# An FFT filter with a mixture of experts behind it: the first block's transposes ordered behind slot 29 of the opening plan

## The chip, the cores and the metric

The kernel runs on one core of a Trainium2 chip. Five engines work in that core, each on an instruction stream of its own, in order: TensorE (PE: matmuls, and transposes as matmuls), VectorE (DVE), ScalarE (ACT), GpSimd (POOL), and SyncE (SP), which here issues nearly all DMAs. An instruction that waits holds up everything behind it on its engine. The metric is the device time of one launch in microseconds; lower is better.

## The reference

Two parts, one after the other. First a spectral filter over the sequence, for 8 batches of 2496 tokens with 256 channels; then a mixture of experts over all 19968 tokens, in which each token goes to two of eight experts:

```python
X = np.fft.rfft(x, axis=1)
Y = X * (filt_r + 1j * filt_i)[None]
x = np.fft.irfft(Y, n=2496, axis=1).reshape(19968, 256)
logits = x @ w_gate
noisy = logits + np.log1p(np.exp(x @ w_noise)) * noise
top2 = two largest of the 8 noisy logits, softmax over the two -> weights
for e in range(8):                       # the tokens that chose e
    h = np.maximum(x[mask] @ w1[e], 0)   # 256 -> 1024
    out[mask] += weight * (h @ w2[e])    # 1024 -> 256
```

## The kernel before

**The filter.** 2496 = 39 x 64, so the transform is two DFTs: one over a (39 points) and one over b (64 points), each a matmul with a table of cosines and sines. One batch passes through `s1` (DFT over a, written to a DRAM scratch `fd`, lines 307 to 327 and 355), `kgl`/`kg0` (reads `fd` back), `kg1` (DFT over b and the product with the filter), `kg2` (inverse over b, into the tile `G`), `t3` (transposes `G`) and `i2` (inverse over a). `i2` (lines 503 to 526) is a matmul (L512) into a PSUM bank, a copy on ScalarE into a tile `yt` (L522), and a DMA of that tile into the DRAM tensor `y` (L526). Each half of a batch's channels takes six such rounds.

**Routing.** From `G` come the gate's logits; `gate` (VectorE, L725 to L827) finds each token's two experts and its rank in the list of each, with three small matmuls (L782 to L784) that need the sums `rs` (L766); `route` writes lists of token rows to DRAM, per expert.

**The experts.** A block is 512 tokens of one expert. `read_list` loads its row numbers, `gather` fetches the rows from `y` with four indirect DMAs on GpSimd (L991), `turn` transposes them: for each half kc of the 256 channels four transposes into one PSUM bank (`xps`, L1007), a copy on ScalarE (L1011) and a difference on VectorE (L1012). Then follow the two layers (lines 120 to 122), whose results are added to `out` by indirect DMAs.

**The order.** Two batches are filtered alone, by a plan written out in slots (`fft_stream`, 32 of them); every instruction of the plan is pinned to the one before it on its engine (`pin`), so that the plan stands in the order written. Slots 26 to 31 also hold the third batch's DFT over a (`s1`, two matmuls of it in each). The experts' blocks start once the first batch is routed, and their instructions are not pinned: the scheduler that builds the program places them between the plan's by its own estimate of times. From then on the generator of the filter and that of the experts run in turn. In the plan's last slots `t3` and `i2` of the second batch share two PSUM banks (tag `yps`, `MOVES[26]`). The first channel half writes its rounds through three tiles in turn, the second half through two:

```python
            yt = P.tile([RP, 4, 128], F32, name="yt", tag=("mxl0", "mxh1", "mxl1")[g0 // 4 % 3], bufs=1)
        else:
            yt = P.tile([RP, 4, 128 + E], F32, name="yt", bufs=2)
```

Outside the functions below, the plan's `s1` entries are these two lines (slot 26 to 31, and what `s1` runs):

```python
        for j in range(11):
            at(26 + j // 2, s1, 22 + j)
```

Of the kernel before, what the change touches and what calls it, by code (L numbers as in the profile page):

```python
# [124 lines left out]
def f32v(ap):  # L125
    return ap.bitcast(F32)
# [3 lines left out]
PACES = 115  # L130
FILL = {0: 0, 1: 14}
RAW = 3
WIDE = 4
FIRSTS = 2
EARLY = {"q1": "hps", "q2": "hps", "q5": "yps", "q6": "yps", "u1": "xps"}
# [5 lines left out]
class Moe:  # L141
    def __init__(self, ctx, tc, io):
        self.tc, self.nc, self.io = tc, tc.nc, io
        nc = self.nc
        self.cp = ctx.enter_context(tc.tile_pool(name="cp", bufs=1))
        self.dp = ctx.enter_context(tc.tile_pool(name="dp", bufs=1, space=DRAM))
        self.y = self.dp.tile([NROW, YW], F32, name="y")
        self.lst = self.dp.tile([NLR, LR], F32, name="lst")
        self.P = ctx.enter_context(tc.tile_pool(name="P", bufs=1))
        self.PS = ctx.enter_context(tc.tile_pool(name="PS", bufs=1, space=PSUM))  # L150
        self.xx, self.early, self.last = {}, True, {}
        self.writes, self.reads = [], []
        self.held = self.held_any = False
        self.banks = dict(EARLY)
        self.setup()
        self.tabs, self.wodd = [], 0
        self.sp = self.spw = self.lasta = None

    def after(self, i):
        return self.tc.issue_after(i.ins) if i is not None else nullcontext()  # L160
# [146 lines left out]
    def s1(self, bt, g0):  # L307
# [4 lines left out]
        x = self.xx.pop((bt, g0))  # L312
        if self.early and bt < RAW:

# [213 lines left out]
    def fft_stream(self):  # L528
# [48 lines left out]
        q = [(n, kg) for n in range(2 * FIRSTS) for kg in range(5)]  # L577
# [56 lines left out]
        for t in range(max(plan) + 1):  # L634
            self.banks.update(MOVES.get(t, {}))
            for g in plan.get(t, []):
                self.pin(g, hold=g.func is not gates)
            if t - 12 in start:
                gating.append(start.index(t - 12))
            if gating:  # L640
                self.pin(self.gating_more, gating[0], hold=False)
                if gating[0] in self.routes:
                    for _ in range(6):
                        self.pin(self.gating_more, gating[0], hold=False)
                    gating.pop(0)

            while self.done_routes < 0 and t >= 14:
                next(rq, None)
            yield -1

        while self.made < 1:
# [346 lines left out]
    def turn(self, xg, nt):  # L998

        nc, P = self.nc, self.P  # L1000
        xT = []
        xg, at = xg
        w = 128 * nt
        for kc in range(2):
            q = self.PS.tile([128, 512], F32, name="xps", bufs=1)
            for t in range(nt):
                nc.tensor.transpose(q[:, t * 128:(t + 1) * 128], xg[t][:, kc * 128:(kc + 1) * 128], self.ident)  # L1007
            h = P.tile([128, 512], R32, name=f"mxh{kc}", bufs=1)
            l = P.tile([128, 512], R32, name=f"mxl{kc}", bufs=1)
            h, l = h[:, :w], l[:, :w]  # L1010
            nc.scalar.copy(h, q[:, :w])  # L1011
            nc.vector.tensor_sub(l, q[:, :w], f32v(h))  # L1012
            xT.append((h, l))
        gate = P.tile([128, 4, 1], F32, name="gt", bufs=3)[:, :nt]
        rows = self.stage[:, 2048:2048 + 8 * YW].rearrange("p (s w) -> p s w", w=YW)[:, at:at + nt, D:]
        nc.gpsimd.tensor_copy(gate, rows[:, :, bass.ds(self.ra, 1)])
        xT.append(gate)
        return xT
# [48 lines left out]
    def expert(self, parts, may, fill=None):  # L1067
# [5 lines left out]
        while self.ahead:  # L1073
# [34 lines left out]
            for t in range(nt):  # L1108


                wide = ready >= WIDE
                if wide or t % 2 == 0:
# [130 lines left out]
```

## Time and profile before

| | |
|---|---|
| median of 3 runs | 2326.6 us (2326.11 to 2327.73) |
| the profiled execution | 2317.03 us, its span 2315.2 us |
| PE busy | 2264.9 us (98%), 13089 matmuls |
| DVE, ACT, POOL busy | 1542.5 (67%), 1189.4 (51%), 937.2 us (40%) |
| mean DMA rate | 142 GB/s; 239 GB/s from 115 to 160 us |
| PE busy from 115 to 160 us | 33.92 of 45 us |

Times in the rows are microseconds from the start of the span. A timeline row gives the start, the time until its last instruction ended, the engine, the line, the operation and what it writes and reads; in brackets stands how long the engine sat idle before it and what ended that. A row of waits gives who waited for whom, the sum, how often, and the longest. `SPq` is SyncE issuing a DMA: its duration is that of the issue, not of the transfer.

### The profile page before, as it was taken

The numbers are of one execution on the slowest core, as the hardware profiler recorded it, in microseconds if no ns is written. First come the engines' busy times: TensorE is split into PE (matmuls) and PEld (weight loads), VectorE is DVE, ScalarE is ACT, GpSimd is POOL, SyncE is SP. The second block draws the span as 40 slices with busy tenths as digits, with TensorE's granted clock in tenths as the row PEclk, the third lists the DMA queues.
The fourth block names the chain that finished last, engine by engine and source line by source line (L and its number), as shares of the span: only waits on it lengthen the run. The fifth ranks groups of instructions, "written<-read, shape, count | busy, mean of one in ns | idle before, by whom it ended". The sixth has DMA issues, their size and how long they took to land. (4 is left out here: it accounts for less than half of the span.)

```text
span 2315.2 us, 39310 instructions
## 1 busy us (share of the span) xinstructions
PE 2264.9 (98%) x13089; PEld 1898.8 (82%) x13089; DVE 1542.5 (67%) x3331; ACT 1189.4 (51%) x2373; POOL 937.2 (40%) x827
## 2 busy tenths in 40 slices
PE   8879999999999999999999999999999999999998
PEld 5448888888888888888888888888888888889997
DVE  4867797678669665875669666854444445557886
ACT  5655656654554554454444444443444344447775
POOL 4014254332435334443434433543535454535442
PEclk9989999999999999999999999999999999999999
DMA  8677757664655555554454553443444445567773
GB/s 238 193 236 193 195 139 200 175 160 120 180 132 130 142 130 131 118 147 120 106 131 104 117 143 87 95 100 88 95 90 94 90 93 128 124 185 224 216 218 87
DMA packets 284723, 329.64 MB, mean 142 GB/s; under 512 B 37371, under 2 KB 197603, under 8 KB 284515
## 3 DMA queue, kind: packets, MB, share of 16 engines
q1 hardware_dynamic: 222435, 241.61, 34.3%
q0 software_dynamic: 62080, 85.47, 21.5%
q8 instruction: 105, 1.72, 0.3%
q14 instruction: 103, 0.84, 0.1%
HBM read 221.98 MB, written 105.78 MB: 142 GB/s over the span
## 5 line engine op out<-in xcount | busy, mean ns | idle before, releaser
L1119 PE MATMUL yps<-w,hh 128*128 128x512 f32 x2112 | 747.3, 398 | 0.0
L1127 POOL DMA_INDIRECT out<-stage,ids x320 | 532.3, 1663 | 264.6 <-DVE stage L1126 121.3
L1120 PE MATMUL yps<-w,hl 128*128 128x256 f32 x2112 | 571.3, 281 | 0.0
L991 POOL DMA_INDIRECT stage<-y,ids x320 | 329.6, 1030 | 584.8 <-PE xps L1007 197.6
L121 PE MATMUL hps<-mxl,w1h 128*128 128x512 f32 (+1 forms) x1424 | 535.0, 376 | 0.0
L122 PE MATMUL hps<-mxh,w1l 128*128 128x512 f32 (+1 forms) x1424 | 528.8, 372 | 0.0
L1095 DVE SCALAR_TENSOR_TENSOR hl<-hps,hh 128x512 fp32r<-128x512 f32 (+1 forms) x712 | 438.6, 630 | 134.6 <-ACT hh L1094 133.2
L120 PE MATMUL hps<-mxh,w1h 128*128 128x512 f32 (+1 forms) x1424 | 523.1, 378 | 3.9 <-DVE hl L1095 3.3
L1094 ACT ACTIVATE hh<-hps 128x512 fp32r<-128x512 f32 (+1 forms) x712 | 381.5, 555 | 239.2 <-PE hps L122 230.2
L1119 PEld LDWEIGHTS yps<-w,hh 128*128 128x128 f32 x2112 | 389.3, 188 | 80.2 <-issue 0.2
L1120 PEld LDWEIGHTS yps<-w,hl 128*128 128x128 f32 x2112 | 397.1, 188 | 18.9 <-DVE w1l L1057 0.6
L122 PEld LDWEIGHTS hps<-mxh,w1l 128*128 128x128 f32 x1424 | 268.1, 188 | 46.7
L120 PEld LDWEIGHTS hps<-mxh,w1h 128*128 128x128 f32 x1424 | 264.9, 188 | 50.0 <-DVE hl L1095 6.5
L121 PEld LDWEIGHTS hps<-mxl,w1h 128*128 128x128 f32 x1424 | 268.2, 188 | 41.4
L1124 ACT ACTIVATE stage<-yps,gt 128x256 f32<-128x256 f32 x320 | 143.8, 476 | 273.0 <-PE yps L1120 235.9
L1126 DVE SCALAR_TENSOR_TENSOR stage<-yps,gt,stage 128x256 f32<-128x256 f32 x264 | 120.9, 479 | 184.6 <-ACT stage L1124 184.2
L1012 DVE TENSOR_TENSOR mxl<-xps,mxh 128x512 fp32r<-128x512 f32 (+1 forms) x178 | 113.0, 635 | 149.7 <-ACT mxh L1011 147.1
L1011 ACT CAST mxh<-xps 128x512 fp32r<-128x512 f32 (+1 forms) x178 | 96.8, 544 | 221.6 <-PE xps L1007 189.5
L963 POOL CAST ids<-lt 128x8 int32<-128x8 f32 (+2 forms) x63 | 15.3, 243 | 379.0 <-DMA lt<-lst 343.8
L1057 DVE TENSOR_TENSOR w1l<-stage,w1h 128x512 fp32r<-128x512 f32 x180 | 123.5, 686 | 58.4 <-ACT w1h L1056 56.6
L1056 ACT CAST w1h<-stage 128x512 fp32r<-128x512 f32 x180 | 111.8, 622 | 93.1 <-PE hps L121 51.8
L1057 DVE TENSOR_TENSOR w<-stage,w 128x512 fp32r<-128x512 f32 x216 | 141.8, 684 | 21.2 <-ACT w L1056 20.8
(222 smaller groups left out, 3075.9 us busy)
## 6 DMA issues: line engine op xcount, KB each, us to landing
stage<-w SPq DMA_DIRECT2D x396, 256.0 KB
x<-x SPq DMA_DIRECT2D x88, 256.0 KB
fd<-c SPq DMA_DIRECT2D x77, 240.0 KB
wb<-w SPq DMA_DIRECT2D x18, 1024.0 KB
fx<-fd SPq DMA_DIRECT2D x140, 128.0 KB
out<-z SPq DMA_DIRECT2D x24, 702.0 KB
y<-yt SPq DMA_DIRECT2D x40, 248.6 KB
y<-yt SPq DMA_DIRECT2D x40, 234.0 KB
```

What stands on the lines that cost most here:

```text
L120: nc.tensor.matmul(o, lh, rh, start=start, stop=False)
L121: nc.tensor.matmul(o, lh, rl, start=False, stop=False)
L122: nc.tensor.matmul(o, ll, rh, start=False, stop=stop)
L991: self.pin(lambda: self.nc.gpsimd.indirect_dma_start(out=x, out_offset=None, in_=self.y[:BLK + ready * ROWS], in_offset=bass.IndirectOffse ...
L1057: nc.vector.tensor_sub(l, sv, f32v(h))
L1094: nc.scalar.activation(h, p, AF.Relu)
L1095: nc.vector.scalar_tensor_tensor(l, p, 0.0, f32v(h), op0=ALU.max, op1=ALU.subtract)
L1119: nc.tensor.matmul(bank, h, hl, start=(f == 0), stop=False)
L1120: nc.tensor.matmul(p, l, hl[:, 0], start=False, stop=(f == 7))
L1124: nc.scalar.activation(o, p, AF.Copy, scale=gate[:, t])
L1126: nc.vector.scalar_tensor_tensor(o, bank[:, 1], gate[:, t], o, op0=ALU.mult, op1=ALU.add)
L1127: a = nc.gpsimd.indirect_dma_start(out=self.io["out"][:BLK + ready * ROWS], out_offset=bass.IndirectOffsetOnAxis(ap=ids[:, t:t + 1], axis= ...
```

## The change

The generator keeps the last matmul pinned at the end of slot 29 as `mark`. The first call of `turn` after that puts its first transpose behind `mark`, and clears it.

```diff
+TURN = 29
...
-        self.sp = self.spw = self.lasta = None
+        self.sp = self.spw = self.lasta = self.mark = None
...
             while self.done_routes < 0 and t >= 14:
                 next(rq, None)
+            if t == TURN:
+
+                self.mark = self.last[self.nc.tensor.engine]
             yield -1
...
             for t in range(nt):
-                nc.tensor.transpose(q[:, t * 128:(t + 1) * 128], xg[t][:, kc * 128:(kc + 1) * 128], self.ident)
+                with self.tc.issue_after(self.mark) if self.mark is not None else nullcontext():
+                    nc.tensor.transpose(q[:, t * 128:(t + 1) * 128], xg[t][:, kc * 128:(kc + 1) * 128], self.ident)
+                self.mark = None
```

Added lines move the numbers: L316, L491, L512 and L1007 of before are L317, L492, L513 and L1012 of the change. `q_1417` and the like are PSUM tiles.

TensorE's stream before, in slots 27 and 28 of the plan (L491 is `t3`, L512 `i2`, L316 `s1`), with the first block's transposes L1007 one by one among them:

```order
L512 MATMUL q_1412<-tf,cm 117x512
L1007 MATMUL xps<-ident,stage 128x128
L491 MATMUL q_1417<-ident,G 120x128 x4
L1007 MATMUL xps<-ident,stage 128x128
L512 MATMUL q_1424<-tf,cm 117x512
L316 MATMUL q_1429<-x,cm 120x512
L316 MATMUL q_1436<-x,cm 120x512
L491 MATMUL q_1442<-ident,G 120x128 x2
L1007 MATMUL xps<-ident,stage 128x128
L512 MATMUL q_1447<-tf,cm 117x512
L1007 MATMUL xps<-ident,stage 128x128
L491 MATMUL q_1452<-ident,G 120x128 x4
```

The same place in the change:

```order
L513 MATMUL q_1412<-tf,cm 117x512
L492 MATMUL q_1417<-ident,G 120x128 x4
L513 MATMUL q_1424<-tf,cm 117x512
L317 MATMUL q_1429<-x,cm 120x512
L317 MATMUL q_1436<-x,cm 120x512
L492 MATMUL q_1442<-ident,G 120x128 x2
L513 MATMUL q_1447<-tf,cm 117x512
L492 MATMUL q_1452<-ident,G 120x128 x4
```

All four transposes of the block's first half are gone from here; the plan's own matmuls stand as before.

Where they stand now, on TensorE at the end of slot 29 (q_1500 and q_1505 are its `s1`); first before:

```order
L512 MATMUL q_1494<-tf,cm 117x512
L316 MATMUL q_1500<-x,cm 120x512
L316 MATMUL q_1505<-x,cm 120x512
L491 MATMUL q_1510<-ident,G 120x128 x4
L512 MATMUL q_1517<-tf,cm 117x512
```

and in the change:

```order
L513 MATMUL q_1494<-tf,cm 117x512
L317 MATMUL q_1500<-x,cm 120x512
L317 MATMUL q_1505<-x,cm 120x512
L1012 MATMUL xps<-ident,stage 128x128 x4
L492 MATMUL q_1510<-ident,G 120x128 x4
L513 MATMUL q_1517<-tf,cm 117x512
```

The four stand together behind the slot's `s1`, ahead of slot 30. The second half's four transposes keep their place behind the first matmuls of the first block. The streams of ScalarE, GpSimd and SyncE are the same as before until about 165 us of the profiled execution, that of VectorE but for a few small swaps from about 144 us. Behind that the scheduler placed some instructions of the first blocks otherwise; TensorE's stream is the same again from its matmul 1413 of 13089, at about 280 us.

## Rows read from the trace of the kernel before

**Rows 1.** Waits of TensorE from 115 to 160 us.

```profile
PE xps L1007 <- DMA stage<-y,ids: 6.5, 2, 4.9
PE q L512 <- ACT yt L522: 2.0, 2, 1.8
PE rk L782 <- DVE rs L766: 0.9, 1, 0.9
```

**Rows 2.** Timeline of TensorE in the plan's slots 27 to 30.

```profile
121.24 1.02 PE L512 MATMUL q<-tf,cm 120*117 120x512 f32 x2
127.17 0.48 PE L1007 MATMUL xps<-ident,stage 128*128 128x128 f32 x1 [4.90 <-DMA stage<-y,ids]
...
130.10 0.48 PE L1007 MATMUL xps<-ident,stage 128*128 128x128 f32 x1 [1.60 <-DMA stage<-y,ids]
130.37 1.91 PE L512 MATMUL q<-tf,cm 120*117 120x512 f32 x2
132.07 3.41 PE L316 MATMUL q<-x,cm 117*120 117x512 f32 x4
...
137.87 1.88 PE L316 MATMUL q<-x,cm 117*120 117x512 f32 x4
...
141.73 1.12 PE L512 MATMUL q<-tf,cm 120*117 120x512 f32 x2
...
150.22 1.12 PE L512 MATMUL q<-tf,cm 120*117 120x512 f32 x2 [1.80 <-ACT yt L522]
```

**Rows 3.** Busy time by engine in stretches: PE, PEld, DVE, ACT, POOL, clock, DMA share, GB/s.

```profile
120.00:125.00 5.00, 2.27 (x9) 0.89 (x7) 4.14 (x11) 2.88 (x7) 2.11 (x3) 0.99 0.39 89
125.00:130.00 5.00, 1.33 (x5) 0.92 (x5) 1.61 (x5) 0.59 (x1) 3.81 (x6) 0.50 1.03 320
130.00:135.00 5.00, 4.90 (x7) 2.12 (x8) 0.00 (x0) 1.17 (x2) 2.47 (x4) 0.50 1.00 351
135.00:140.00 5.00, 4.87 (x21) 2.62 (x19) 2.52 (x13) 3.95 (x8) 0.19 (x1) 0.99 0.93 287
140.00:145.00 5.00, 3.87 (x18) 2.11 (x17) 4.83 (x32) 2.83 (x7) 0.00 (x0) 1.00 0.86 266
145.00:150.00 5.00, 3.41 (x18) 1.59 (x16) 4.86 (x35) 2.46 (x6) 0.00 (x0) 1.00 0.94 272
150.00:155.00 5.00, 4.78 (x25) 2.40 (x25) 2.39 (x15) 3.95 (x10) 0.00 (x0) 1.00 0.56 154
```

**Rows 4.** Timeline of ScalarE: copies of `i2`, and the first block's first cast.

```profile
122.30 0.58 ACT L522 COPY yt<-q 117x512 f32<-117x512 f32 x1
...
132.32 0.58 ACT L522 COPY yt<-q 117x512 f32<-117x512 f32 x1 [3.15 <-PE q L512]
...
139.48 0.37 ACT L522 COPY yt<-q 117x256 f32<-117x256 f32 x1 [0.18 <-DMA y<-yt]
...
149.58 0.58 ACT L522 COPY yt<-q 117x512 f32<-117x512 f32 x1 [2.10 <-DMA y<-yt]
...
157.60 0.60 ACT L1011 CAST mxh<-xps 128x512 fp32r<-128x512 f32 x1
```

**Rows 5.** Timeline of SyncE: writes to `y` (x2 starts with the first of two).

```profile
123.42 0.38 SPq L526 DMA_DIRECT2D y<-yt  x1
...
129.54 4.23 SPq L526 DMA_DIRECT2D y<-yt  x2
...
144.17 1.53 SPq L526 DMA_DIRECT2D y<-yt  x2
```

**Rows 6.** Timeline of VectorE, the second batch's gate.

```profile
135.79 0.12 DVE L421 MEMSET G<- 128x80 f32 x1 [9.04 <-PE q L491]
...
140.57 0.46 DVE L766 TENSOR_REDUCE rs<-rank 117x8 f32<-117x176 f32 x1
```

**Rows 7.** Timeline of GpSimd: the copy that needs all four gathers of the first block.

```profile
133.42 0.19 POOL L1016 COPY gt<-stage 128x4 f32 x1 [0.53 <-DMA stage<-y,ids]
```

**Rows 8.** Busy time by engine, from the first blocks to where the streams agree again.

```profile
175.00:275.00 100.00, 97.75 (x643) 85.05 (x641) 74.76 (x122) 60.22 (x119) 40.84 (x37) 1.00 0.72 187
```

## The prediction, as it was put on record

> **What bounds the kernel now.** I read the page first: TensorE is busy 98% of the span, so a change can only win where TensorE idles, and can lose wherever it is made to. Then the waits of TensorE around the place of the change [rows 1]: from 115 to 160 us two waits for gathered rows, 6.5 us in sum, are by far the largest. The timeline of TensorE [rows 2] shows them: the first transpose idles 4.90 us behind the matmul that ends at 122.26, the second 1.60 us. The plan's own `t3` and `i2` stand behind these transposes and wait with them. The clock falls too [rows 3]: the granted share is 0.50 from 125 to 135 us, which is the lower level, 1.2 GHz, after the 4.90 us of idling; it is 0.99 again from 135 us, after 4.90 us of work in 5. The reader is to see in rows 2 what that costs: slot 27's four `s1` matmuls take 3.41 us, slot 28's 1.88.
>
> That is the tempting reading. The other view is of what else moves in these same microseconds. The DMA engines are full: share 1.03, 1.00 and 0.93 from 125 to 140 us, then 0.86 and 0.94 to 150 [rows 3]. And ScalarE's copies of `i2`, which hand data to the DMAs, show waits for them [rows 4].
>
> **What goes.** Two waits of 4.90 + 1.60 = 6.50 us [rows 2]. With the clock kept up, 3.41 - 1.88 = 1.53 us on `s1` and 1.91 - 1.02 = 0.89 us on the `i2` at 130.37 would go as well, 2.42 together. The most that the change can bring is 8.9 us.
>
> **What is added.** Nothing is added, four transposes move. They took 0.48 us each where the clock was low, and stand now behind slot 29's `s1`. By the second set of four (kc = 1, in one bank as well) they are some 0.6 us at most, and they fall ahead of a wait of 1.80 us at 150.22 [rows 2] with nothing but four plan steps between, so this wait hides them; without that cover they cost 0.6 us. What they feed is ScalarE's cast at 157.60 [rows 4], over 10 us behind their new place, and all four gathers have landed by 133.42 [rows 7]. So the moved wait does not come back at the new place: neither the block nor the gathers are late. No DMA moves in this stretch, on SyncE or on GpSimd.
>
> **What is late next.** This is the step on which the forecast rests. `i2` needs a PSUM bank, which the previous `i2`'s copy (L522) frees; the copy needs a `yt` tile, which the write to `y` of three rounds earlier frees (three tiles in turn). Count the copies of this half: the third is at 122.30, the fourth at 132.32, the sixth at 139.48 [rows 4]. The sixth takes the third one's tile. The third's write was issued at 129.54 [rows 5], 6.7 us after its copy had ended and with no wait of SyncE for TensorE between: SyncE was working off the weight loads and writes queued ahead of it, into engines that were full. It landed 9.9 us later, and the sixth copy waited 0.18 us for it [rows 4]. So in the kernel before the copy came 0.18 us too early, at a time when TensorE had lost 6.5 us. A TensorE that is earlier arrives earlier at the same landing. The queue ahead of that write is unchanged, and the engines' share of 1.03 and 1.00 leaves no room to bring it forward; I take 139.4 us for it in the change too.
>
> ScalarE works in order, so nothing behind the sixth copy passes 139.4. The next `i2`, the one at 141.73 [rows 2], needs the bank that it frees at 139.4 + 0.4 = 139.9, as an estimate. Before, it stood behind the rank matmuls, which waited for `rs` until 141.03 [rows 1, 6]. VectorE reaches `rs` 5.2 us after the memset of `G` at 135.79, which itself sat 9.04 us waiting for slot 28's `t3` [rows 6]. In the change that `t3` comes at about 122.3 + 0.6 + 1.0 + 1.9 = 125.8, so `rs` is ready well before 139.9, even with some 5 us of waiting for the ScalarE step on the way. The gain is thus pinned at 141.73 - 139.9 = 1.8 us there. The waits of TensorE for gathers become waits of `i2` for copies: the fourth copy for the first write (issued 123.42), the fifth for the second, the sixth for the third.
>
> **The second pin.** The same happens once more with the second half's two tiles. The copy at 149.58 waited 2.10 us for a write issued at 144.17 [rows 4, 5], a landing of 5.3 us. If that landing keeps its 5.3 us and the issue comes 1.8 us earlier, the gain passes through whole. If the engines deliver by their own rate (share 0.86 and 0.94, not quite full), the write lands when it did, and the gain is 0. Between 0 and 1.8 I take 1.4: the engines have some room there, so nearer to the upper end, less a little for a clock that may be low after the wait that ends at 139.9. From 150 us on the share is 0.56 [rows 3] and nothing pins: ScalarE, TensorE and the first block follow as they stand.
>
> **What the reordering further on does.** From about 165 to 280 us some instructions of the first blocks stand otherwise. TensorE leaves 100 - 97.75 = 2.25 us unused from 175 to 275 [rows 8]. That bounds what a better order can win. For a worse one I take the same size on the other side, as an estimate, and 0 as the value: a few swaps between work of the same kind. Behind 280 us the stream is the same, TensorE is never out of work for long, and what was gained at 160 us stays until the end.
>
> **Sum.** -1.4 us in the opening, 0 behind it. On the profiled execution's own 2317.03 us (span 2315.2 and 1.8 around it) that is 2315.6. The runs' median of 2326.6 lies 9.6 us above the profiled execution; I put the difference on it: 2325.2 us. This case's own range is from -1.8 - 2.3 to +2.3, that is 2322.5 to 2328.9.
>
> **Rivals.**
>
> *The stall goes and stays gone* (0.19). The writes to `y` are no bound, because the third write is issued earlier once SyncE's queue moves, or lands earlier. For it: the waits in rows 1 are TensorE's largest, and the idle DMA stretch from 120 to 125 us (share 0.39) shows room. Against it: the 0.18 us at 139.48, and a queue that was already issuing when the stall began. It would give up to 6.50 + 2.42 = 8.9 us, 2317.7; half-way cases, with a landing 3 to 4 us earlier, lie at 2320 to 2322.
>
> *The clock turns it into a loss* (0.13). In the change TensorE no longer idles once for 4.90 us, but several times: for the fourth, fifth and sixth copy, for `rs`, and last for up to 3 us before 139.9. If the clock is then low and the thin work of slots 29 to 31 doesn't bring it back, the busy 3.87 + 3.41 + 4.78 = 12.1 us from 140 to 155 [rows 3] grow by the ratio of rows 2, 3.41 / 1.88, so by 9.8 us. Of this the idle time of these three stretches hides 15 - 12.1 = 2.9 and the gain at 139.9 another 1.8: +5.1 us, 2331.7. It decides at 140 to 150: before, the granted clock there was 1.00 at a busy share of 0.68 to 0.77, which speaks against it. The Trainium skill, in "TensorE: Matmul & The Clock Gate", section "A second HAM failure mode: psum-queue depth-cycling", describes such a case, in which small idle times between groups of matmuls that wait for PSUM banks make the clock go down and up again. The rows of 140 to 150 us, where TensorE works in that way and the clock is full, don't agree with it; that it would be met only after a longer wait no run here shows yet.
>
> That the change doesn't do what it says is excluded by the order: all four transposes have left slots 27 and 28, and TensorE's stream there is otherwise the same.
>
> **Chances.** The likeliest case has 0.68. A difference within 0.2% (4.65 us) is about what a measurement of this kernel can't tell from none. The likeliest case's own range lies inside that bound but for its edge, so it gives 0.67 of "same" and 0.01 of "faster"; the first rival's cases from 4.65 to 8.9 us make "faster", with the edge, 0.20; the second rival makes "slower" 0.13. Eighty in a hundred reach from 2318.8, which takes in the half-way cases of the first rival, to 2330.6 on the other side, where the loss would have begun.
>
> **What would show it.** The waits of `xps` for `stage<-y,ids` are gone from 115 to 160 us. In their place stand waits of TensorE's `i2` for copies, and of the copies L522 for the DMA `y<-yt`, three of them before 140 us, 6 us or more in sum. The sixth copy is again at 139 to 140 us. VectorE's memset of `G` comes near 127 us instead of 135.79. The first cast of the first block comes 1 to 2 us before 157.60. The forecast is wrong if the sixth copy is before 137 us (then the first rival), or if the granted clock at 140 to 150 us is near 0.5 (then the second), or if TensorE loses more than 5 us from 175 to 275 us (then the reordering, which I put at nothing).

## The result, and the profile after

The change makes the kernel slower by 0.2%: 2331.25 us in the median of 20 runs (2326.56 to 2335.86) against 2326.56 us of 20 runs before; ratio 1.0019, 95% interval 1.0012 to 1.0025. The forecast was 2325.2 us and "same", with a range of its own of 2322.5 to 2328.9; the measured median lies 2.35 us above that range. The profiled execution has a span of 2327.6 us (2329.43 us with what lies around it). The one of before (2315.2 us) was a lucky execution: it lies 9.6 us under its median, so the two spans can't be subtracted. Stretches of them can.

In the opening the change does what the forecast said. Waits of TensorE, the kernel after, 115 to 160 us, where before had [rows 1]:

```profile
PE q L513 <- ACT yt L523: 4.0, 2, 3.2
PE q L513 <- issue: 3.2, 2, 3.1
```

The waits for gathered rows are gone; waits for `i2`'s bank stand in their place. (`issue` is idle time for which the profile names no releaser. The longest of it, 3.06 us, ends at 127.09, where the copy at 126.45 below has just ended.) Timeline of TensorE after, slots 27 to 30, for [rows 2]:

```profile
127.09 2.06 PE L513 MATMUL q<-tf,cm 120*117 120x512 f32 x2 [3.06 <-issue]
...
137.92 1.12 PE L513 MATMUL q<-tf,cm 120*117 120x512 f32 x2 [3.15 <-ACT yt L523]
...
147.60 1.12 PE L513 MATMUL q<-tf,cm 120*117 120x512 f32 x2 [0.80 <-ACT yt L523]
```

ScalarE after, the copies of `i2` and the first block's first cast, for [rows 4]:

```profile
126.45 0.58 ACT L523 COPY yt<-q 117x512 f32<-117x512 f32 x1 [4.65 <-DMA y<-yt]
129.53 0.59 ACT L523 COPY yt<-q 117x512 f32<-117x512 f32 x1 [1.24 <-issue]
137.50 0.37 ACT L523 COPY yt<-q 117x256 f32<-117x256 f32 x1 [5.38 <-DMA y<-yt]
...
146.96 0.58 ACT L523 COPY yt<-q 117x512 f32<-117x512 f32 x1 [1.10 <-DMA y<-yt]
...
155.03 0.60 ACT L1017 CAST mxh<-xps 128x512 fp32r<-128x512 f32 x1
```

SyncE after, for [rows 5], with a write of zeros to `out` that will matter, and VectorE's memset, for [rows 6]:

```profile
128.12 0.49 SPq L291 DMA_DIRECT2D out<-z  x1
128.70 3.75 SPq L527 DMA_DIRECT2D y<-yt  x2
...
142.14 1.48 SPq L527 DMA_DIRECT2D y<-yt  x2
```

```profile
124.75 0.12 DVE L422 MEMSET G<- 128x80 f32 x1
```

This execution is 1.97 us ahead of that of before already at 110 us, where nothing differs. With that added, the sixth copy starts at 139.47 us: before, at 139.48 [rows 4]. The pin that the forecast named holds. That it holds to a hundredth is luck: in the change's second profile the copy starts at 139.94. The `i2` behind it starts at 139.89 in the time of before, where the forecast had 139.9.

Busy time by engine after, columns as in [rows 3], the last for [rows 8]:

```profile
125.00:130.00 5.00, 2.91 (x6) 1.30 (x6) 1.24 (x5) 2.31 (x5) 3.85 (x5) 0.60 1.04 336
130.00:135.00 5.00, 4.60 (x17) 2.71 (x16) 3.21 (x15) 2.09 (x4) 1.13 (x2) 0.72 0.95 346
135.00:140.00 5.00, 1.73 (x6) 0.89 (x7) 4.76 (x37) 2.44 (x6) 0.19 (x1) 0.96 0.97 293
140.00:145.00 5.00, 5.00 (x16) 2.58 (x15) 1.97 (x9) 2.46 (x5) 0.00 (x0) 0.70 0.92 275
145.00:150.00 5.00, 4.20 (x18) 1.91 (x17) 1.80 (x16) 2.86 (x7) 0.00 (x0) 1.00 0.78 224
...
175.00:275.00 100.00, 96.64 (x624) 84.74 (x622) 70.51 (x112) 56.46 (x111) 38.87 (x37) 0.97 0.71 179
```

Behind both waits of 3 us the granted clock falls to its lower level, 1.2 GHz, for part of the time. From 175 to 275 us TensorE leaves 3.36 us unused, not 2.25 [rows 8]. What is new there is one wait, and behind 275 us a second. First near 190 us, on TensorE and on ScalarE after:

```profile
191.70 0.79 PE L391 MATMUL q<-th,hl 128*128 128x512 f32 x1 [3.37 <-issue]
```

```profile
190.55 0.62 ACT L379 CAST th<-fx 128x512 fp32r<-128x512 f32 x1 [6.69 <-issue]
191.07 0.58 ACT L360 COPY c<-q 120x512 f32<-120x512 f32 x1
```

The same work before, which no row ahead of the prediction shows:

```profile
189.21 0.59 ACT L359 COPY c<-q 120x512 f32<-120x512 f32 x1 [1.43 <-PE q L326]
193.85 0.62 ACT L378 CAST th<-fx 128x512 fp32r<-128x512 f32 x1 [4.05 <-DMA fx<-fd]
```

```profile
192.60 0.40 PE L390 MATMUL q<-th,hl 128*128 128x512 f32 x1
```

Before, the copy `c<-q` stands ahead of the cast that waits for its read; after, behind it. TensorE's matmul starts at 191.70, where that copy ends (191.07 + 0.58 = 191.65). The profile names no releaser here; in that of `zero_later` (below) the same wait, 3.39 us, is put down to this copy, and in that of `early_reorder` ScalarE's wait, 6.08 us, to `fx<-fd`. The clock is low behind the wait in this profile: 0.79 and 0.63 us a matmul, not 0.40.

Second, near 285 us, SyncE, ScalarE, VectorE and TensorE after:

```profile
274.99 0.42 SPq L291 DMA_DIRECT2D out<-z  x1
275.62 3.78 SPq L1034 DMA_DIRECT2D stage<-w  x4
```

```profile
281.99 0.62 ACT L1062 CAST w1h<-stage 128x512 fp32r<-128x512 f32 x1 [3.99 <-DMA stage<-w]
```

```profile
283.37 1.29 DVE L1101 SCALAR_TENSOR_TENSOR hl<-hps,hh 128x512 fp32r<-128x512 f32 x2
```

```profile
284.12 0.50 PE L120 MATMUL hps<-mxh,w1h 128*128 128x512 f32 x1 [1.52 <-DVE hl L1101]
```

And before, SyncE, ScalarE and TensorE:

```profile
275.00 0.57 SPq L290 DMA_DIRECT2D out<-z  x1
275.78 3.30 SPq L1028 DMA_DIRECT2D stage<-w  x4
```

```profile
281.33 0.62 ACT L1056 CAST w1h<-stage 128x512 fp32r<-128x512 f32 x1 [3.16 <-DMA stage<-w]
```

```profile
283.63 0.39 PE L120 MATMUL hps<-mxh,w1h 128*128 128x512 f32 x1
```

ScalarE waits for the same weights before, behind the same zeros, but TensorE had other matmuls meanwhile and shows no idle time. In the change's order some of these stand earlier; that this is what uncovers the wait is read from the two timelines and not tested alone.

This second wait lies inside the reordered stretch. In the two traces TensorE's streams are the same again from the 1614th matmul, at 310 us before and 312 us after, and not from 280 us. The last matmuls that stand elsewhere are the third batch's rank matmuls, ahead of a run of `yps` matmuls before and behind it after; TensorE before, then after:

```profile
308.57 0.20 PE L784 MATMUL rk<-small,rs 117*8 117x1 f32 x2
...
309.74 0.28 PE L122 MATMUL yps<-w,hl 128*128 128x256 f32 x1
```

```profile
311.09 0.28 PE L122 MATMUL yps<-w,hl 128*128 128x256 f32 x1
...
311.64 0.20 PE L788 MATMUL rk<-small,rs 117*8 117x1 f32 x2
```

### The profile page after: what moved, and what is told of

It is laid out like the page before. It is cut to its first block, busy times and chain, and to the rows that moved or that the text cites. A ratio compares the mean times of both kernels' runs of the same rounds, so it can differ in the third digit from the quotient of the medians.

```text
span 2327.6 us, 39307 instructions
## 1 busy us (share of the span) xinstructions
PE 2270.4 (98%) x13089; PEld 1901.3 (82%) x13089; DVE 1542.8 (66%) x3331; ACT 1188.8 (51%) x2373; POOL 925.6 (40%) x827
## 5 line engine op out<-in xcount | busy, mean ns | idle before, releaser
L1133 POOL DMA_INDIRECT out<-stage,ids x320 | 525.8, 1643 | 285.7 <-DVE stage L1132 130.1
```

What stands on the lines that cost most here:

```text
L1133: a = nc.gpsimd.indirect_dma_start(out=self.io["out"][:BLK + ready * ROWS], out_offset=bass.IndirectOffsetOnAxis(ap=ids[:, t:t + 1], axis= ...
```

## The experiments

Instructions bear the same names in both builds, so an order can be held: ahead of the last loop each engine's instructions are chained in a list read from a build, and parts of lists can be exchanged. Beyond such an order, and writes of zeros moved where that is said, each kernel is that of before; the change and before themselves ran again as they are. The excerpts of lists below have the line numbers of before.

```diff
+        self.more_order()
         with self.tc.If(self.more < E * CAPB * BLK // UNIT):
...
+    def more_order(self):
+        ...
+            for a, b in zip(row, row[1:]):
+                if a.engine == b.engine:
+                    self.tc.add_manual_dep(b, a.name, ...NoSync...)
```

The runs came in five groups on their own chips, each with runs of before beside them (medians 2327.8, 2314.3, 2314.6, 2320.5 and 2315.4 us), so ratios are compared. The table gives them, and from one profile each where TensorE stands against the first profile of before: the end of the last matmul of a point up to which both kernels have done the same matmuls, minus the same in before, 0 at 110 us; negative is ahead. "Zeros" are the writes to `out` at 129 and 138 us (early; 702 and 468 KB) and at 275 us (late; 702 KB). In names with `zero31` and `zero25` the early ones are moved to that slot, in `zero_later` the late one behind the weight loads, in names with `zeros` both.

```
                  ratio   95%              151   174   216   261   289   334 us
before again      0.9994  0.9980-1.0008   -1.1  -2.5  -0.1  -0.1   1.5   3.1
early_reorder     1.0011  1.0001-1.0021   -1.1  -2.5  -1.6  -1.6  -1.5  -1.5
late_reorder      1.0026  1.0015-1.0037   -0.3  -2.2  -3.1  -3.1  -0.5  -0.5
reorder_alone     1.0025  1.0013-1.0038    0.0  -1.4   1.7   1.6   4.3   5.8
open_alone        1.0004  0.9990-1.0017   -0.1  -0.6   2.8   2.8   2.8   4.2
the change        1.0019  1.0012-1.0025   -0.7  -2.7   0.5   0.5   2.7   4.2
the change again  1.0013  1.0002-1.0025   -0.6  -2.3   0.2   0.2   5.2   6.9
after_lists       1.0035  1.0021-1.0048    0.0  -0.9   0.6   0.6   5.1   6.4
after_swap        1.0022  1.0013-1.0031   -1.2  -2.4  -3.1  -3.1   3.0   3.0
zero_later        1.0006  0.9997-1.0015   -0.1  -1.3   1.9   1.9   1.9   1.9
before_zero25     1.0010  1.0001-1.0018    2.2   1.6   1.4   1.4   1.4   1.4
open_zero31       1.0015  1.0005-1.0026   -3.8   2.3   1.5   1.5   1.5   1.5
open_zero25       0.9990  0.9980-0.9999   -3.9  -4.7  -4.8  -4.8  -4.8  -4.8
open_zeros        0.9987  0.9977-0.9996   -3.3  -3.9  -3.8  -3.8  -3.8  -3.8
after_zero25      1.0025  1.0016-1.0035   -3.1  -4.4  -4.1  -4.2   1.8   1.9
after_zeros       1.0004  0.9995-1.0013   -4.2  -5.8  -3.9  -4.0  -1.9  -0.5
after_zeros_swap  0.9986  0.9977-0.9994   -3.9  -5.5  -6.4  -6.4  -6.3  -6.3
```

A column of one profile scatters by some 2 to 3 us (before again is 2.5 ahead at 174 and 3.1 behind at 334), so what follows leans on groups of rows.

**The opening or the reordering.** `open_alone` is the order of before with the four transposes moved; `reorder_alone` the order of the change with them put back.

```diff
 PE L316 q<-x,cm      (slot 29)
+PE L1007 xps<-ident,stage x4
 PE L491 q<-ident,G   (slot 30)
...
-PE L1007 xps<-ident,stage   (four, in slots 27 and 28)
```

> The kernel before with the four transposes of the first block's first half moved to where the change has them, behind slot 29's s1, and every other instruction of every engine held in the order of the kernel before. Theory A (what was gained by 174 us is lost at one place, where TensorE, now some 3 to 5 us earlier, runs into a read-back of fd that has not landed, idles 3 to 4 us there and works at 1.2 GHz for some us behind it): that wait, q of the third batch's DFT over b near 190 us, is there, and the time is that of the change, 2329.5 to 2333 (ratio 1.001 to 1.003). Theory B (the scheduler's reordering behind 165 us, above all the two list reads lt ahead of the fd and fx reads in SyncE's stream, makes the wait): no wait over 2 us at that place, the opening's gain of 1.5 to 3 us stays, and the time is 2323.5 to 2326 (0.9987 to 0.9998).

> The order of the change on every engine, but with the four transposes put back to slots 27 and 28, where the kernel before has them. Theory A (the opening's lead causes the loss): the gather waits are back, TensorE comes to the third batch's DFT over b 3 to 5 us later and finds fd landed, and the time is that of the kernel before, 2325.5 to 2328 (0.9995 to 1.0006). Theory B (the reordering behind 165 us causes it): the wait near 190 us stands although the opening has gained nothing, and the time is that of the change or above, 2331 to 2334 (1.0019 to 1.0033).

> The changed kernel once more, for a second profile. If the 3.4 us of idling before the third batch's DFT over b near 190 us and the 6.8 us at 1.2 GHz there belong to the program, both are in this profile too. If the further losses behind 500 us (3.3 us at 610 us, 1.2 GHz at 600 and 611 us), where the streams of both kernels agree, belong to the one execution, they are not at the same places. The time is 2330 to 2332.5 (1.0012 to 1.0025).

> The kernel before against itself, for a second profile and for the scatter: ratio 0.9993 to 1.0007. The profile is a longer execution than the first (that was 2317.0 us, 9.6 below the median): if it was a lucky one, the waits that make the difference lie behind 280 us and not in the stretch from 115 to 200 us, where the gather waits of 4 to 7 us in sum and no wait over 2 us near 190 us are expected again.

TensorE in `reorder_alone` and in `open_alone`:

```profile
193.85 0.79 PE L392 MATMUL q<-th,hl 128*128 128x512 f32 x1 [3.15 <-issue]
```

```profile
196.53 1.36 PE L429 MATMUL q<-cf,a 128*128 128x128 f32 x8 [1.87 <-issue]
```

Theory B holds: the reordering without the opening has the loss (1.0025) and the wait, the opening without it has neither that wait nor a measurable loss. Its interval reaches 1.0017, though, and its one profile loses 3.3 us from 174 to 216 us too, with the wait shown as the longest, so this run alone doesn't show the opening to be free. The opening's gain did not stay, against theory B's number: at 151 us the six profiles with the transposes moved and the early zeros in place are 0.45 us ahead on average, the five with the old place 0.5. The moved transposes gain nothing there. Both waits of the change are there again in its second profile (2.91 us at 192, 2.14 at 286). The low clock near 190 us is not: behind that wait the granted clock is 1.00 from 185 to 205 us. The losses that the first showed at 600 to 611 us are no part of it: the second profile of before has such a wait too, 3.62 us for `u<-G,wg` at 614 us.

**Which part of the reordering.** The lists cut at 217 us.

```diff
-order of before on every engine
+early_reorder: order of the change up to 217 us, then that of before
+late_reorder: order of before up to 217 us, then that of the change
```

> The transposes at their old place; the order of the change from 146 to 217 us, and the order of the kernel before ahead of and behind that. Theory C (the loss of the change lies behind 270 us, where the first blocks' matmuls now stand closer behind weights that are still on their way; what it loses near 190 us the kernel before loses a little later as well): time as before, 2326.5 to 2329 (ratio 0.9995 to 1.0006), with the wait of 3 us for q near 192 us in the profile all the same, and TensorE level with the kernel before at 216 us. Theory D (the wait near 190 us and the lower clock behind it are the loss): 2331 to 2334 (1.0014 to 1.0030).

> The transposes at their old place; the order of the kernel before up to 217 us, and that of the change behind it. Theory C: the whole loss is here, 2331 to 2334 (1.0014 to 1.0030): no wait over 2 us near 190 us, but 1.5 to 2.5 us of idling for hl near 285 us and 3 us or more lost between 270 and 310 us. Theory D: time as before, 2326.5 to 2329 (0.9995 to 1.0006).

The larger loss is behind 217 us, as theory C said (the two intervals overlap, but both profiles agree); its wait for `hl` is there with 2.19 us, at 281.66. But the early part isn't free (1.0011, interval above 1), so D is not wholly wrong.

**The late place: zeros ahead of weights.**

```diff
 SP L526 y<-yt
-SP L290 out<-z       (702 KB, 275 us)
 SP L1028 stage<-w  x4
+SP L290 out<-z
```

> The order of the change on every engine, with one edit: the 702 KB write of zeros to out that SyncE issues at 275 us stands behind the four weight loads that follow it. If the idling of TensorE for hl near 285 us comes from weights that land late behind this write (ScalarE's cast w1h waits 4.0 to 4.8 us for them, then VectorE's hl, then TensorE), that wait falls to under 0.5 us, ScalarE's to under 3 us, and the time is 1.5 to 2.5 us below the change's, 2329 to 2330.5 (1.0005 to 1.0012 of before). If the loads are late for another reason (the engines are full, or the slot of the buffer comes free late), both waits and the time stay, 2331 to 2333 (1.0013 to 1.0022).

It came out as expected. SyncE and ScalarE in `zero_later`:

```profile
277.76 2.14 SPq L1030 DMA_DIRECT2D stage<-w  x4
279.94 0.41 SPq L292 DMA_DIRECT2D out<-z  x1
```

```profile
281.98 0.62 ACT L1058 CAST w1h<-stage 128x512 fp32r<-128x512 f32 x1 [1.37 <-DMA stage<-w]
```

From the issue of the loads to the cast are 4.2 us, against 6.4 in the change: 2.2 us less, what 702 KB take at the 320 GB/s of [rows 3]. TensorE shows no wait there. In the seven profiles with the change's late order and the zeros ahead it loses 4.2 us on average from 261 to 289 us, in the seven with the order of before 0.2, in the three of the change's order with the zeros behind 0.7.

**The opening's pin: zeros ahead of a write to y.**

```diff
-            at(24 + i, self.zero_out, 1, i)
+            at(24 + i if i < 2 else 31, self.zero_out, 1, i)   # open_zero31
+            at(24 + min(i, 1), self.zero_out, 1, i)   # ..._zero25, ..._zeros
```

> The transposes moved as in the change, every other order that of the kernel before, but the last two writes of zeros to out for the second batch (702 KB and less) in slot 31, behind the writes to y, and not ahead of the third and fifth of them. It tests the step that named the write to y as the next limit of the opening. If so: the third write to y is issued 1 us earlier and lands some 3 us earlier (702 KB at 320 GB/s are 2.2 us), the sixth copy of the second batch's i2 comes at 137 to 138 us and not at 139.4 to 140.4 us, TensorE's longest wait there falls from 3.0 us to about 1, and the first cast of the first block comes 1 to 2 us earlier. If the pin is a rate of the full engines: the copies stay within 0.5 us. The time differs from the opening alone (2328.7) by -2 to +2, since the zeros now lie ahead of the first block's loads of w at 158 us: 2326.5 to 2330.5 (0.9995 to 1.0012).

ScalarE's copies and TensorE in `open_zero31`:

```profile
138.08 0.37 ACT L524 COPY yt<-q 117x256 f32<-117x256 f32 x1 [2.78 <-DMA y<-yt]
...
145.30 0.59 ACT L524 COPY yt<-q 117x512 f32<-117x512 f32 x1 [0.22 <-PE q L514]
```

```profile
167.47 2.08 PE L120 MATMUL hps<-mxh,w1h 128*128 128x512 f32 x4 [7.39 <-ACT mxh L1013]
```

The sixth copy came only 0.9 us earlier (138.08, and 0.48 for this execution's start), but the second pin went altogether, and TensorE was 3.8 us ahead at 151. Then weights landed late behind the zeros in their new place, ScalarE waited 8.4 us for them, and 6 us were lost: 1.0015, outside what was expected. So the zeros went the other way, to slot 25, where SyncE has issued them all by 118 us:

> The kernel before, order and all, but the last two writes of zeros to out for the second batch (702 KB and less) are issued in slot 25 with the other zeros, in the idle stretch of the DMA engines before 120 us, and not at 129 and 138 us among the gathers and the writes to y. The transposes stay at their old place. Theory W (these zeros, ahead of the third write to y, are what pins the opening whichever place the transposes have): the copies no longer wait for y<-yt near 139 and 149 us, but TensorE still waits for the gathers, 4 to 7 us in sum, so it gains 1 to 2 us by 151 us: ratio 0.9990 to 1.0000. Theory P (the pin is the engines' rate over the whole stretch): nothing moves by more than 0.5 us; 0.9996 to 1.0006.

> The transposes moved as in the change, every other order that of the kernel before, and the two writes of zeros in slot 25. Theory W: the sixth copy comes at 138.5 us or earlier in the time of the kernel before, the copies behind it don't wait for y<-yt, TensorE is 3 to 4 us ahead at 151 us as in the run with the zeros in slot 31, and now nothing takes it back at 167 us, since the zeros are out of the way of the weights: ratio 0.9982 to 0.9995. Theory F (a lead of TensorE is given back at the read-backs of fd between 175 and 216 us whatever its size): 3 to 4 us ahead at 174 us and within 1 us of the kernel before at 216 us; ratio 0.9996 to 1.0006.

> The change's order on every engine and the two writes of zeros in slot 25. The loss behind 270 us stays (1.8 to 4 us near 285 us, under theory C), the opening gains 3 to 4 us by 151 us. Theory W: 1 to 3 us below the change, 1.0000 to 1.0012 of before. Theory F: as the change, 1.0012 to 1.0022, with a wait for q near 190 us of 5 us or more in place of 3.

> As the one with the transposes moved, the order of the kernel before and the zeros in slot 25; besides, the 702 KB of zeros at 275 us stand behind the four weight loads that follow. In the order of the kernel before that wait of ScalarE costs TensorE 0 to 1.6 us, so this brings 0 to 1 us more: ratio 0.9978 to 0.9995 under theory W, 0.9992 to 1.0004 under theory F. Of these four the fastest, if theory W holds.

With the order of before theory W holds: the lead of 4.8 us goes through to the end, and `open_zeros`, 0.9987, beats both kernels. With the change's order it does not: the whole lead and more, 6.0 us, goes at 281 to 289 us, and 1.0025 is above what either theory gave. W's number for `before_zero25` was wrong in sign, because the read of the row numbers that the gathers need (`lt<-lst`) now stands behind the zeros: SyncE issues it at 124.08 us, before at 120.10, and GpSimd starts on the gathers 5.3 us later. TensorE and GpSimd in that kernel, and GpSimd before:

```profile
133.91 0.48 PE L1009 MATMUL xps<-ident,stage 128*128 128x128 f32 x1 [10.92 <-DMA stage<-y,ids]
```

```profile
127.09 0.21 POOL L965 CAST ids<-lt 128x4 int32<-128x4 f32 x1 [11.00 <-DMA lt<-lst]
```

```profile
121.78 0.18 POOL L963 CAST ids<-lt 128x4 int32<-128x4 f32 x1 [6.42 <-DMA lt<-lst]
```

So moving the transposes is worth something: with the zeros in slot 25, 1.0010 against 0.9990.

**Is that all, and what makes the wait near 190 us.**

```diff
 after_zeros: order of the change, zeros as in open_zeros
 after_lists: order of the change, SyncE up to 205 us as before
```

> The change's order on every engine; the two writes of zeros of the second batch in slot 25, and the 702 KB of zeros at 275 us behind the four weight loads that follow. If late weights behind these zeros are the whole loss behind 217 us: the wait for hl near 281 us (2.9 us with the zeros ahead) is under 0.5 us, the 4.1 us that the change with the zeros in slot 25 is ahead of the kernel before at 216 us are still there at 330 us, less 0.5 at most, and the ratio is 0.9985 to 1.0000, against 1.0025 with the zeros ahead of the weights. If the order behind 217 us loses by something else as well: less than 2 us ahead at 330 us, ratio 1.0003 to 1.0015.

> The change, with SyncE's stream up to 205 us in the order of the kernel before: the second list read then stands behind the fd write again, and the fd and fx reads come earlier against the list reads. Every other engine as in the change. Theory L (the list reads delay the fx read, and so th and TensorE near 190 us): the wait for q there falls from 2.9 to 3.4 us to under 1.5 us, and the time by 1 to 2 us, to 1.0006 to 1.0016. Theory M (the place of the matmul in TensorE's stream, one step nearer to its read-back, causes it): the wait stays at 2.5 us or more, and the time with it, 1.0011 to 1.0025.

The wait near 281 us goes in `after_zeros` and 0.0021 of the ratio with it, but 3.5 us of the lead at 261 us are lost by 334 us, in waits of 1.5 us and less, so the first answer was too simple. Theory L falls: with the list reads put back TensorE waits 2.70 us (the ratio, 1.0035 from five runs, is above what either theory gave). The ScalarE rows above name the other candidate, an exchange of two instructions; `after_swap` and `after_zeros_swap` undo it in the change and in `after_zeros`:

```diff
 ACT L1124 stage<-yps,gt
-ACT L320 xh<-x
 ACT L1124 stage<-yps,gt
-ACT L378 th<-fx
+ACT L320 xh<-x
 ACT L359 c<-q
+ACT L378 th<-fx
```

> The change, but in ScalarE's stream near 188 us the copy c<-q stands ahead of the cast th<-fx again, as before (and beside it a cast xh ahead of a copy to stage). Theory S (the copy frees the PSUM bank that the next q needs, and stands behind a cast that waits 6 us for the read of fd): the wait of TensorE for q near 190 us falls from 2.7 to 3.4 us to under 1 us, and 1 to 2 us come of it: ratio 1.0004 to 1.0018. If the place of the matmul in TensorE's own stream causes it: the wait stays over 2 us; 1.0011 to 1.0025.

> The change's order with the three writes of zeros out of the way (1.0004 of before) and the same exchange on ScalarE. Theory S: TensorE keeps its lead of 5 to 6 us at 174 us to 216 us within 1 us, and the time falls by 1 to 2 us against the run without the exchange: ratio 0.9993 to 1.0002. What the order behind 217 us still loses in small waits (2 us at 273 us, 2 us from 289 to 334 us) stays, so it does not reach the 0.9987 of the order of before with the same zeros. If not S: 1.0000 to 1.0010.

ScalarE and TensorE near 190 us in `after_swap`:

```profile
186.48 0.59 ACT L361 COPY c<-q 120x512 f32<-120x512 f32 x1 [1.07 <-DMA fd<-c]
191.94 0.62 ACT L380 CAST th<-fx 128x512 fp32r<-128x512 f32 x1 [4.87 <-DMA fx<-fd]
```

```profile
190.01 0.40 PE L392 MATMUL q<-th,hl 128*128 128x512 f32 x1
```

The wait is gone and TensorE is 3.1 us ahead at 216 us, as theory S said; TensorE's own order is that of the change, so it isn't the cause of this wait. The time was not better: the late place took 6.1 us in place of 2.2 to 5. ScalarE and TensorE there, in `after_swap`:

```profile
282.21 0.62 ACT L1058 CAST w1h<-stage 128x512 fp32r<-128x512 f32 x1 [5.99 <-DMA stage<-w]
```

```profile
284.33 0.61 PE L120 MATMUL hps<-mxh,w1h 128*128 128x512 f32 x1 [3.52 <-DVE hl L1097]
```

With the zeros away as well nothing is left of the loss: 0.9986, better than expected, and 6.3 us ahead at 334 us. The small waits of `after_zeros` behind 261 us are absent, so they don't belong to the order as such. Whether the exchange or the single execution took them away is open.

## Why the prediction was wrong

**What goes, what is added, the first pin: right.** The gather waits went, the transposes cost nothing that shows, the memset of `G` came at 126.7 us in the time of before (forecast near 127), three waits of copies before 140 us make 11.3 us (6 or more; the profile puts one of them down to "issue"), and the sixth copy stayed at 139.47. In the nine further profiles with the early zeros in place it starts at 139.2 to 140.6 us in the time of before, with the transposes in either place. The forecast took the queue ahead of the write as given; it did not see the 702 KB of zeros directly ahead of it, SyncE before:

```profile
129.00 0.44 SPq L290 DMA_DIRECT2D out<-z  x1
```

The rival that the stall goes and stays gone is refuted as long as the zeros stand there. Once they don't, about half of it holds: a lead of 4.8 us of its 8.9 in `open_zero25`, with the sixth copy at 137.56.

**The second pin: right step, too large a gain.** The forecast took 1.4 us of a possible 1.8, with an issue of the write 1.8 us earlier. That issue came at 142.14, which is 144.11 in the time of before, so 0.06 us earlier; only the landing was shorter (4.8 us, before 5.4). The copy behind it came 0.65 us earlier in the profile, the first cast 0.6, not 1 to 2, and over the groups nothing is left at 151 us.

**What the reordering does: the step that failed.** It said that the 2.25 us that TensorE leaves unused [rows 8] bound what a better order can win, took the same size for a worse one, and 0 as the value. Idle time bounds a gain only. What a worse order can lose are waits of other engines that TensorE does not see yet, and those stood in the trace of before, outside the rows that were read: ScalarE's 4.05 us for `fx<-fd` at 193.85 and its 3.16 us for `stage<-w` at 281.33. The reordering let TensorE run into both: it put a copy that TensorE needs behind the first, and the second is no longer covered. It costs 1.0025 by itself (1.0013 to 1.0038), some 5.8 us; in the profiles 2.1 us on average from 174 to 216 us (eight with the copy behind the cast; ten with it ahead: 0.2, but up to 3.3 in one) and 4.2 from 261 to 289. The step had a second fault: it took the stream as the same again behind 280 us, and so looked for a loss from 175 to 275 us alone. The streams agree only from 310 us, and the larger wait stands between. By the forecast's own sign, more than 5 us lost from 175 to 275, the reordering would have passed: TensorE loses 3.3 us there from 174 to 261.

**The clock rival: its mechanism, not its place or price.** The granted clock was 0.70 from 140 to 145 us, after an idle time of 3.15 us; the forecast had allowed "a little" for that, and it was full again, 1.00, from 145 us. At 151 us it had cost nothing that shows, with the second pin behind it. The Trainium skill, "TensorE: Matmul & The Clock Gate", section "A second HAM failure mode: psum-queue depth-cycling", has TensorE idling often and briefly between groups of matmuls as it goes through PSUM banks, and its clock going down and up. With rows of 125 to 145 us at 0.60, 0.72, 0.96 and 0.70 the trace agrees on the clock, but behind two single waits of 3 us and not behind many short ones. Where it did cost was behind the two waits that the reordering brought, and not each time: near 190 us in the change's first profile (0.79 and 0.87 from 185 to 205 us), not in its second, and near 285 us in `after_swap` (0.85 from 285 to 295 us), where a wait of 3.52 us stands in a loss of 6.1.

What remains unsettled: the two orders can't be told apart once the zeros are away and the pair is exchanged (0.9986 and 0.9987), so which of the swaps behind 217 us took the cover from the weights near 285 us was not looked for. Beside TensorE's and VectorE's, ScalarE's are open: before, its copy `yt<-q` at 272.76 stands ahead of two casts of `w`, in the change behind them, and in SyncE's stream the write to `y` that needs this copy stands ahead of the zeros and the loads.

## What to carry to other kernels

When an edit lets a scheduler place other instructions anew, don't price that at nothing: list every wait of the engines beside the bottleneck that does not show on it yet, since each can become a loss once its cover moves (here waits of 4.05 and 3.16 us became idle times of TensorE of 2.2 to 3.4 and 1.5 to 3.5 us). A lead of the bottleneck engine lives only until the next landing that doesn't move with it; here three stood in a row (a write to `y`, a read-back in front of a bank's copy, a load of weights), and removing one handed the gain to the next. Look in the DMA queue ahead of such a landing for bulk that nobody waits for: moving two writes of zeros, 702 and 468 KB, let the moved matmuls bring what they could not alone (with the zeros moved, 1.0010 without the moved transposes and 0.9990 with them).

## What the runs showed of the hardware

- ScalarE takes its instructions in order: in the change it idled 6.69 us at a cast waiting for a read, a copy of 0.58 us behind it started at 191.07, and TensorE waited for that; with the two exchanged the copy started at 186.48. The Trainium skill, "Perfetto Trace Analysis", section "Tensor Engine Instruction (MATMUL, LD_WEIGHTS)", says so of ScalarE, VectorE and GpSimd; the trace agrees for ScalarE.
- A write of 702 KB ahead of four weight loads on the same issuing engine delayed them by 2.2 us at 275 us (6.4 us from issue to cast against 4.2). And zeros issued earlier moved gathers that GpSimd issues, by way of the read of their row numbers: 10.9 us of waiting, not 4.9.
- Executions of one kernel on one chip scatter by 5 to 15 us over twelve runs (4.9 in `before_zero25`, 15.5 in `open_alone`). The two profiles of before are 15.6 us apart, and the shorter lacks a wait that the longer has: near 285 us TensorE idled 1.4 us in the second and not at all in the first.
